# Down projection by 2x2 block products in seven pairs of the first half, with the rest rows' low parts on GpSimd

## The chip, the cores and the metric

The kernel runs on one core of a Trainium2 chip. The time is that of one execution on the device, in microseconds (us); the median of three runs is compared. The engines are named as in the profile: PE is TensorE, DVE VectorE, ACT ScalarE, POOL GpSimd, SP the engine that issues most transfers. PEld is PE's loading of weights.

## The reference

Two branches read the same x (2048 tokens, 576 features) and are mixed by a gate for each token. All is float32.

```python
def _B_ref(x, W_gate, W_up, W_down):            # 576 -> 4608 -> 576
    gate = jnp.einsum("bsd,df->bsf", x, W_gate)
    up = jnp.einsum("bsd,df->bsf", x, W_up)
    gate = gate * (lambda x, dt: x.astype(dt))(gate > 0, gate.dtype)
    h = gate * up
    return jnp.einsum("bsf,fd->bsd", h, W_down)

x = A_x
g = _sigmoid((x * gate_w).sum(-1, keepdims=True))
a = _A_ref(x, A_wqkv, A_w_phi, A_wo)            # linear attention with 32 heads
b = _B_ref(x, B_W_gate, B_W_up, B_W_down)
return g * a + (1 - g) * b
```

The change lies in branch B, the gated layer: two projections up to 4608 features, a product, and the down projection back to 576.

## The kernel before

**Precision.** A float32 operand is split into a high part (rounded by ACT to the type that PE takes at full rate) and a low part (the difference, made by DVE: source minus high part). A product is then three matmuls: high by high, high by low, low by high.

**Stages.** The first 340 us of the span or so are attention. Then come 72 units, and a short tail. The 4608 features are 36 chunks of 128; the tokens are two halves of 1024, each of two blocks t of 512. Units 0 to 35 take the chunks with the first half's tokens, units 36 to 71 with the second's (`units`, L855). Two units with neighbouring chunks are a pair g; there are NG = 18 pairs in a half. Unit u belongs to pair u // 2; the first unit of a pair is called even, the second odd.

**A unit** makes gate and up for one chunk and 1024 tokens by seven block products in place of eight (Strassen's scheme in Winograd's form), on pre-added operands. `step(u, j)` (L1322 and on) issues one of them: `product` puts seven 512-column matmuls on a bank of PSUM, in the order 1, 5, 6, 2, 7, 3, 4 for j = 0 to 6. The text counts steps from 1, so product 4 is step 7. Products 1, 6, 7, 4 accumulate one after another on a bank cx, 5 and 3 on ca, 2 on cy, and between them ACT and DVE read the running sums: ACT copies cx and ca aside (g1, u2, g2), DVE adds cy, cx and ca to the copies (L1413, L1415, L1418; L1415 is the add of cx to u2, which has to be over before product 4 goes on the same bank), and `gated` (L1290) makes h from gate and up, one block of 512 tokens at a time.

**The weights of the products** are made in the first half, one unit ahead (`make` in `step`), and stored in HBM for the second half. For unit v = u + 1: ACT makes the high parts of three weight blocks (L864, in `blocks`) at j = 0, DVE their low parts (L867, 128x768) and the low part of the rest rows (`low_w_rows`, L870, 32 partitions x 384) at j = 1; at j = 2 DVE adds the blocks up in place in four instructions (`sums_of_blocks`, L885 to L888), which have to wait for the readers of the old values; ACT makes those sums' high parts at j = 3, DVE the low parts (L867 128x1024 and L870 32x512) at j = 4. SP stores the two tiles at j = 2 and j = 5 (L1393, L1400). In the second half SP loads them again instead.

**The down projection** of pair q is issued while pair q + 1 is computed: after the product of step j, `step` appends the s-th down product, s = 7 * odd + j. It lands on one of two banks, pd0 and pd1, in turn, and DVE adds the bank to the sums in SBUF one step later (`add_up`). The output's 576 features are four blocks of 128, taken as i, m, and 64 rest rows on banks of their own (pm).

- First half, plain (`plain_down`, `down_plain`): eight products of two chunks by three matmuls, and the rest rows in 8 matmuls. Each of the pair's four hidden blocks (two chunks, two token blocks) has a high part (`high_h`, L1233) and a low part (`low_h`, L1238). The pair's weights come in with `load_down` (L908), and their parts are made in its odd unit, at j = 2 and 3 (L1091, L1094).
- Second half but for its last pair, by blocks (`prepare_down`, `down`): for each m seven products of the 2x2 block scheme with three matmuls each, and the rest rows in 8 matmuls. The hidden blocks and their differences (`minus`, L1287) make seven operands, each with a high and a low part; the weights' blocks are added up by POOL in place (`down_sums_of_blocks`, L1080 to L1083) and split in two steps for each m, m = 0 in the pair's odd unit and m = 1 in the next even one. After each of the 14 products DVE adds the bank to a sum (L1206).

**Other work on DVE in the first half.** `second_half` scales the second half's tokens and adds up their operands on DVE, one instruction of 128x768 (L335, L341) at the end of each unit from unit 4, until it is done.

**Order.** `in_order` around the units holds PE, DVE, ACT, POOL and SP to the order in which `step` issues. Within a step it is: the product, the add of the last down product, the hidden parts, the weights for the next unit, the copies and adds of gate and up, the down weights, the next down product.

Of the kernel before, what the change touches and what calls it, by code (L numbers as in the profile page):

```python
# [7 lines left out]
F32 = mybir.dt.float32  # L8
# [75 lines left out]
def gated_mix_kernel(  # L84
# [26 lines left out]
    SUB, ADD, MULT = ALU.subtract, ALU.add, ALU.mult  # L111
    tt, pt = nc.vector.tensor_tensor, nc.gpsimd.tensor_tensor
# [98 lines left out]
    with tc.tile_pool(name="ps_v", bufs=1, space=PSUM) as ps_v:  # L211
# [7 lines left out]
        for k in range(5):  # L219
            w = raw.tile([P, TB + VW], F32, name="xwv", tag="raw")  # L220
# [428 lines left out]
    t = NT - 1  # L649
# [203 lines left out]
    NG = NC // 2  # L853
# [3 lines left out]
    def load_w(u):  # L857
        if units[u][0] == 0:
            RAW[u] = wraw.tile([P, 4, 3, P], F32, name="wr")
            nc.sync.dma_start(RAW[u], wgu[units[u][1]])  # L860
# [5 lines left out]
    def low_w(o, a):  # L866
        tt(out=o[:, :, 3:5], in0=a[:, :, 0:2], in1=o[:, :, 0:2].bitcast(F32), op=SUB)  # L867

    def low_w_rows(o, a):
        tt(out=o[64:96, :, 2], in0=a[64:96, :, 2], in1=o[64:96, :, 2].bitcast(F32), op=SUB)  # L870

    WB, WS = {}, {}

    def blocks(u, f):

        if u not in WB:
            o = WB[u] = wop.tile([P, 3, 5, P], F32R, name="wb")
            WO[u] = {1: (o, 0), 2: (o, 1), 4: (o, 2)}
        f(WB[u], RAW[u][:, 0:3])
# [10 lines left out]
    def block_sums(u, f):  # L890
        if u not in WS:
            o = WS[u] = wop.tile([P, 4, 5, P], F32R, name="ws")
            WO[u].update({5: (o, 2), 6: (o, 0), 7: (o, 3), 3: (o, 1)})
        f(WS[u], RAW[u])
# [164 lines left out]
    WD, W4, HID, ACC, ACC4, BANK, REST = {}, {}, {}, {}, {}, {}, {}  # L1059
# [36 lines left out]
    def rest_weights(g, step):  # L1096

        a = WDR[g][:, 8 * P:].rearrange("p (c q) -> p c q", c=2)
        if step == 0:
            nc.scalar.activation(W4[g][:, 0:2, 0], a, AF.Copy)  # L1100
        elif step == 1:
            tt(out=W4[g][:, 0:2, 1], in0=a, in1=W4[g][:, 0:2, 0].bitcast(F32), op=SUB)
            pt(out=a[:, 0], in0=a[:, 0], in1=a[:, 1], op=ADD)
        elif step == 2:
            nc.scalar.activation(W4[g][:, 2, 0], a[:, 0], AF.Copy)
            nc.scalar.activation(W4[g][:, 3], W4[g][:, 1].bitcast(F32), AF.Copy, scale=-1.0)
        else:
            tt(out=W4[g][:, 2, 1], in0=a[:, 0], in1=W4[g][:, 2, 0].bitcast(F32), op=SUB)
# [21 lines left out]
    def rows(i, m, t, hf):  # L1130
        r = (2 * i + m) * P
        return slice(r, r + P), slice((2 * hf + t) * TB, (2 * hf + t + 1) * TB)
# [5 lines left out]
    def load_rest(hf):  # L1138
        for t in range(2):
            a = ACC4[hf, t] = sums_of[t][:64, 2]  # L1140
            nc.sync.dma_start(a, att[4 * P:, rows(0, 0, t, hf)[1]])

    PLAIN = {1: (0, 0, 1), 2: (0, 1, 1), 3: (2, 0, 1), 4: (0, 0, 0), 5: (0, 1, 0), 6: (2, 0, 0),
             8: (1, 0, 1), 9: (1, 1, 1), 11: (1, 0, 0), 12: (1, 1, 0)}

    def down_plain(g, s):

        if s not in PLAIN:
            return lambda: []
        i, m, t = PLAIN[s]  # L1150
        first, last = g == 0, g == NG - 1
# [25 lines left out]
            return []  # L1177
        return add

    def down(g, s, bank):  # L1180

        first, last = g == NG, g == 2 * NG - 2
        m, i = divmod(s, 7)
        n = DOWN[i]
        key = 0 if n in (1, 6, 7, 4) else 1
        if n in (1, 5, 2):
            BANK[m, key] = bank(m, n)
        ps = BANK[m, key]
        h, l = HID[g, n]
        o, k = WD[g, m], PLACE[n]  # L1190
        mm = lambda ps, w, v, a, z: nc.tensor.matmul(ps, w, v, start=a, stop=z, skip_group_check=True)  # L1191
        mm(ps, o[:, 0, k], h, n in (1, 5, 2), False)
        mm(ps, o[:, 0, k], l, False, False)
        mm(ps, o[:, 1, k], h, False, True)
        if m == 0 and n in (1, 5, 2, 4):
            w, r = {1: (0, 0), 5: (2, 1), 2: (1, 0), 4: (3, 1)}[n]
            if first and n in (1, 5):
                REST[r] = pm.tile([P, TB], F32, name=f"pm{r}")
            w = W4[g][:, w].rearrange("p s q -> p (s q)")
            mm(REST[r], w, h, first and n in (1, 5), False)  # L1200
            mm(REST[r], w, l, False, last and n in (2, 4))

        def add():
            i, t = ADDS[n]
            a = ACC[1, i, m, t]
            tt(out=a, in0=ps, in1=a, op=ADD)  # L1206
            return []
        return add
# [22 lines left out]
    def high_h(key, src):  # L1231
        h, l = hp.tile([P, TB], F32R, name="hh"), hp.tile([P, TB], F32R, name="hl")
        nc.scalar.activation(h, src, AF.Copy)  # L1233
        HID[key] = h, l

    def low_h(key, src):
        h, l = HID[key]
        tt(out=l, in0=src, in1=h.bitcast(F32), op=SUB)  # L1238
# [34 lines left out]
    def add_up():  # L1273

        if len(STORED) > 2:
            for hf, i, m, t in STORED.pop(0):
                if hf == 0:
                    load_acc(1, i, m, t)
        if PEND:
            done.extend(PEND.pop()())  # L1280
        store(done)
        STORED.append(tuple(done))
        done.clear()

    def minus(a, b):

        tt(out=b, in0=a, in1=b, op=SUB)  # L1287
# [11 lines left out]
    def bank(n):  # L1299

        pool, name, new = {1: (px, "cx", 1), 6: (px, "cx", 0), 7: (px, "cx", 0), 4: (px, "cx", 0),
                           5: (pa, "ca", 1), 3: (pa, "ca", 0), 2: (py, "cy", 1)}[n]
        if new:
            BANKS[name] = pool.tile([P, TB], F32, name=name)
        return BANKS[name], bool(new)
# [16 lines left out]
    def step(u, j):  # L1322


        g, odd = divmod(u, 2)
        v, q = u + 1, g - 1
        plain, was_plain = g < NG or g == 2 * NG - 1, q < NG
        ps, first = bank(SEQ[j])
        product(ps, u, SEQ[j], first)
        add_up()  # L1330
        make = 0 < u < NC - 1
        cx, ca, cy = (BANKS.get(n) for n in ("cx", "ca", "cy"))
        old = not odd and g > 0

        if j == 0:
            if u > 0:
                last_cx, a = LATE.pop()
# [5 lines left out]
        e2, e1, o2, o1 = ODD[q] if old else EVEN[g] + (None, None) if odd else [None] * 4  # L1343
        if odd and plain or old and was_plain:
            key, x2, x1 = ((g, 0), e2, e1) if odd else ((q, 1), o2, o1)
            if j == 0:
                high_h(key + (1,), x2)
            elif j == 1:
                high_h(key + (0,), x1)
                low_h(key + (1,), x2)  # L1350
            elif j == 2:
                low_h(key + (0,), x1)
        elif odd:
            if j == 1:
                high_h((g, 1), e1)
            elif j == 3:
                low_h((g, 1), e1)
                minus(e2, e1)
            elif j == 4:
                high_h((g, 5), e1)  # L1360
            elif j == 5:
                low_h((g, 5), e1)
        elif old:
            if j == 0:
                high_h((q, 6), e1)
                minus(o2, e2)
            elif j == 1:
                high_h((q, 3), o2)
                low_h((q, 6), e1)
            elif j == 2:  # L1370
                low_h((q, 3), o2)
                high_h((q, 7), e2)
                high_h((q, 2), o1)
            elif j == 3:
                minus(o1, e1)
                low_h((q, 7), e2)
            elif j == 4:
                high_h((q, 4), e1)
                low_h((q, 2), o1)
            elif j == 5:  # L1380
                low_h((q, 4), e1)

        if make:
            if j == 0:
                blocks(v, high_w)
                if v + 1 < NC:
                    load_w(v + 1)
            elif j == 1:
                blocks(v, low_w)
                blocks(v, low_w_rows)  # L1390
            elif j == 2:
                if v < NC - 2:
                    nc.sync.dma_start(wbd[v], WB.pop(v).bitcast(F32))  # L1393
                sums_of_blocks(v)
            elif j == 4:
                block_sums(v, low_w)
                block_sums(v, low_w_rows)
            elif j == 5:
                if v < NC - 2:
                    nc.sync.dma_start(wsd[v], WS.pop(v).bitcast(F32))  # L1400
        elif j == 0 and NC < u < 2 * NC - 1:
            load_operands(v)
# [13 lines left out]
        elif j == 6:  # L1416
            a = T["g2"]
# [5 lines left out]
            w = WO.pop(u)  # L1423
# [9 lines left out]
            prepare_down(g, 0, j)  # L1433
        elif old and not was_plain:
            prepare_down(q, 1, j)
        if old and j == 5:
            load_down(g)
        if old and j == 6:
            ODD.pop(q)
# [26 lines left out]
                store_rest(0, 1)  # L1466
                load_rest(1)
        if j == 6 and u < NC:
            if u >= 4:
                next(later_half, None)  # L1470
            if u == NC - 3:
                for _ in later_half:
                    pass
                load_operand(1, 0)
                load_operand(1, 1)

    later_half = second_half()
    with in_order(tc, nc, nc.tensor, nc.vector, nc.scalar, nc.gpsimd, nc.sync):
# [4 lines left out]
        g = 2 * NG - 1  # L1483
# [149 lines left out]
```

## Time and profile before

| | |
|---|---|
| median of three runs | 1589.73 us (1588.61 to 1591.07) |
| profiled execution | 1589.56 us, its span 1587.8 us |
| granted TensorE clock | 0.997 |
| DVE busy in one pair of the first half (440.60 to 475.50 us of the span) | 27.93 of 34.90 us |
| DVE busy in one pair of the second half (1099.15 to 1132.70 us) | 24.82 of 33.55 us |
| POOL busy in the same two stretches | 0.00 and 4.31 us |

A row of a timeline or of the chain begins with its start and its length in us, counted from the span's start. Then come the engine, the line of the kernel, the operation, what it writes and reads (a tile's number is left out, so that cx stands for all its buffers), the shapes and the count. In square brackets stand the engine's idle time just before and what ended it. A row of a group of instructions has the count, then the total busy time in us and the mean of one in ns, then the idle time before them. An engine's instructions are pipelined: the next one starts before the recorded end of the last, so the time from start to start is what an instruction costs in a queue.

### The profile page before, as it was taken

What the parts mean: (1) busy time and instruction counts of PE and PEld (TensorE: products, weight loads), DVE (VectorE), ACT (ScalarE), POOL (GpSimd) and SP (SyncE); (2) the same over time, 40 slices, a digit from 0 to 9 for tenths busy, and PEclk for the clock granted to TensorE, in tenths of its full rate; (3) what the DMA queues carried; (4) which work ended last, traced back from release to release, by engine and by line L of the source; (5) the groups of instructions that cost most, each with busy time, mean ns of one, the idle gap of its engine ahead of it and who ended that gap; (6) DMA issues with size and microseconds to landing.
All of it is one profiled execution on the core that took longest, in us unless ns stands there. A gap on an engine that the chain in (4) does not pass through costs nothing.

```text
span 1587.8 us, 20181 instructions
## 1 busy us (share of the span) xinstructions
PE 1570.8 (99%) x7823; PEld 1313.4 (83%) x7823; DVE 1190.8 (75%) x1865; ACT 559.0 (35%) x918; POOL 175.2 (11%) x243
## 2 busy tenths in 40 slices
PE   9999999999999999999999999999999999999998
PEld 9999995677888888888888888888888888888887
DVE  4997774577778777787777777777777777777777
ACT  4344335554333333333333334232233232222321
POOL 0126521110000000000000002111111111111110
PEclk9999999999999999999999999999999999999999
DMA  5365315587655576555554516543343343443432
GB/s 171 108 207 192 143 55 157 170 332 261 217 219 211 209 262 223 215 191 221 193 196 183 210 71 233 189 177 143 143 180 143 146 175 131 167 168 131 180 140 75
DMA packets 64539, 283.38 MB, mean 178 GB/s; under 512 B 6802, under 2 KB 17298, under 8 KB 55740
## 3 DMA queue, kind: packets, MB, share of 16 engines
q1 hardware_dynamic: 61228, 270.34, 47.0%
q0 software_dynamic: 2352, 10.11, 2.0%
q10 hardware_dynamic: 864, 1.65, 0.3%
q8 instruction: 61, 1.00, 0.3%
q14 instruction: 34, 0.28, 0.0%
HBM read 172.07 MB, written 108.60 MB: 177 GB/s over the span
## 4 chain that ended last, share of the span: by engine, by line
PE 95%; DVE 3%; ACT 1%; DMA 0%; issue 0%; POOL 0%; SPq 0%; ACTq 0%; POOLq 0%
PE cx L1128 29%; PE ca L1128 14%; PE pd L1168 12%; PE pd L1191 10%; PE cy L1128 7%; PE kv L175 4%; PE pk L175 3%; PE pq L175 3%; PE pm L1168 2%; PE pm L1191 2%; PE kv L421 1%; PE po L562 1%; PE pv L237 1%; PE pw L175 1%; PE ptr L379 1%; PE psf L259 1%
## 5 line engine op out<-in xcount | busy, mean ns | idle before, releaser
L1233 ACT ACTIVATE hh<-g 128x512 fp32r<-128x512 f32 x195 | 120.0, 624 | 458.5 <-DVE g L1290 289.2
L1206 DVE TENSOR_TENSOR ac<-pd,ac 128x512 f32<-128x512 f32 x238 | 164.1, 689 | 144.0 <-PE pd L1191 143.9
L1128 PE MATMUL cx<-xo,ws 128*128 128x512 f32 x1008 | 253.5, 391 | 3.3 <-ACT g L1294 3.3
L1128 PE MATMUL ca<-xo,ws 128*128 128x512 f32 x1008 | 251.9, 389 | 0.0
L1128 PE MATMUL cx<-xo,wb 128*128 128x512 f32 x1008 | 249.0, 389 | 1.5 <-DVE u L1415 1.5
L1128 PEld LDWEIGHTS cx<-xo,ws 128*128 128x128 f32 x1008 | 190.2, 189 | 43.3 <-ACT g L1294 3.7
L1128 PEld LDWEIGHTS cx<-xo,wb 128*128 128x128 f32 x1008 | 188.2, 188 | 42.5 <-DVE u L1415 1.9
L1128 PEld LDWEIGHTS ca<-xo,ws 128*128 128x128 f32 x1008 | 189.2, 188 | 39.3
L1168 PE MATMUL pd<-hh,wd 128*128 128x512 f32 x576 | 200.7, 389 | 0.0
L1191 PE MATMUL pd<-hh,wd 128*128 128x512 f32 x476 | 185.2, 389 | 0.0
L1174 DVE TENSOR_TENSOR ac<-pd,ac 128x512 f32<-128x512 f32 x144 | 99.1, 688 | 105.8 <-PE pd L1168 103.3
L1238 DVE TENSOR_TENSOR hl<-g,hh 128x512 fp32r<-128x512 f32 x195 | 135.7, 696 | 1.9 <-ACT hh L1233 0.2
L1294 ACT ACTIVATE g<-cx 128x512 f32<-128x512 f32 x144 | 85.0, 590 | 130.8 <-PE cx L1128 130.7
L1128 PE MATMUL cy<-xo,wb 128*128 128x512 f32 x504 | 127.3, 392 | 0.0
L1168 PEld LDWEIGHTS pd<-hh,wd 128*128 128x128 f32 x576 | 108.1, 188 | 22.6
L1091 ACT ACTIVATE wd<-wdr 128x384 fp32r<-128x384 f32 (+1 forms) x106 | 62.3, 606 | 143.4 <-DMA wdr<-wd 143.4
L1128 PEld LDWEIGHTS cy<-xo,wb 128*128 128x128 f32 x504 | 95.6, 190 | 20.0
L1168 PE MATMUL pd<-hl,wd 128*128 128x512 f32 x288 | 112.0, 389 | 0.0
L1191 PEld LDWEIGHTS pd<-hh,wd 128*128 128x128 f32 x476 | 89.3, 188 | 18.6
L1191 PE MATMUL pd<-hl,wd 128*128 128x512 f32 x238 | 92.6, 389 | 0.0
L831 POOL TENSOR_TENSOR xo<-xr,xo 32x512 fp32r<-32x512 f32 x5 | 8.3, 1669 | 615.9 <-ACT xo L847 615.9
L864 ACT ACTIVATE ws<-wr 128x1536 fp32r<-128x1536 f32 x36 | 53.7, 1491 | 46.6 <-DVE wr L888 46.6
(256 smaller groups left out, 2574.1 us busy)
## 6 DMA issues: line engine op xcount, KB each, us to landing
wsd<-ws SPq DMA_DIRECT2D x34, 1280.0 KB
ws<-wsd SPq DMA_DIRECT2D x34, 1280.0 KB
wbd<-wb SPq DMA_DIRECT2D x34, 960.0 KB
wb<-wbd SPq DMA_DIRECT2D x34, 960.0 KB
wr<-wgu SPq DMA_DIRECT2D x36, 768.0 KB
wdr<-wd SPq DMA_DIRECT2D x36, 576.0 KB
eT<-et SPq DMA_DIRECT2D x10, 594.0 KB
xt<-xb SPq DMA_DIRECT2D x7, 768.0 KB
```

Of the source, the lines that this page charges most:

```text
L175: nc.tensor.matmul(ps, w, m, start=i == 0, stop=i == len(pairs) - 1)
L237: nc.tensor.matmul(pv[i][c], m, w_[:, k, cs], start=k == 0 and n == 0, stop=k == 4 and n == 1)
L864: nc.scalar.activation(o[:, :, 0:3], a, AF.Copy)
L1091: nc.scalar.activation(o[:, 0], a, AF.Copy)
L1128: nc.tensor.matmul(ps, w, v, start=first and m == 0, stop=m == len(pairs) - 1, skip_group_check=True)
L1168: nc.tensor.matmul(ps, w, v, start=k == 0 and (i < 2 or first), stop=k == len(mms) - 1 and (i < 2 or last), skip_group_check=True)
L1174: tt(out=a, in0=ps, in1=a, op=ADD)
L1191: mm = lambda ps, w, v, a, z: nc.tensor.matmul(ps, w, v, start=a, stop=z, skip_group_check=True)
L1206: tt(out=a, in0=ps, in1=a, op=ADD)
L1233: nc.scalar.activation(h, src, AF.Copy)
L1238: tt(out=l, in0=src, in1=h.bitcast(F32), op=SUB)
L1294: nc.scalar.activation(a, ps, AF.Copy)
```

## The change

Pairs 3, 5, 7, 9, 11, 13 and 15 of the first half (`BY_BLOCKS`) take the down projection by blocks, as the second half does; the pairs between them stay plain. The rest rows keep their plain form in the first half: a table `REST_OF` names the down product with which a rest matmul pair goes, the weights' slot and the hidden operand, and the one operand that the seven lack for it (the even chunk's second token block) gets a high and a low part of its own, under the key 8.

In the odd unit of such a pair and in the two units after it, GpSimd makes the low parts of the product weights' rest rows (L870) in place of DVE. DVE's sums of the blocks and SP's stores then wait for GpSimd.

The load of such a pair's down weights is issued at j = 1 of its even unit in place of j = 5; for the plain pair after it, it stays at j = 5, behind the blocks pair's last low part of down weights, which reads the same tile. `second_half` skips the unit after a pair by blocks.

```diff
-    def low_w_rows(o, a):
-        tt(out=o[64:96, :, 2], in0=a[64:96, :, 2], in1=o[64:96, :, 2].bitcast(F32), op=SUB)
+    def low_w_rows(o, a, f=tt):
+        f(out=o[64:96, :, 2], in0=a[64:96, :, 2], in1=o[64:96, :, 2].bitcast(F32), op=SUB)
+
+    def low_w_rows_aside(o, a):
+        low_w_rows(o, a, pt)
...
             tt(out=W4[g][:, 0:2, 1], in0=a, in1=W4[g][:, 0:2, 0].bitcast(F32), op=SUB)
-            pt(out=a[:, 0], in0=a[:, 0], in1=a[:, 1], op=ADD)
+            if g >= NG:
+                pt(out=a[:, 0], in0=a[:, 0], in1=a[:, 1], op=ADD)
+        elif g < NG:
+            return
...
+    BY_BLOCKS = range(3, NG - 2, 2)
+
+    def is_plain(g):
+        return g < NG and g not in BY_BLOCKS or g == 2 * NG - 1
...
+    REST_OF = ({1: (0, 0, 1), 5: (0, 1, 8), 3: (1, 1, 3), 2: (1, 0, 2)},
+               {1: (0, 0, 1), 5: (2, 1, 5), 2: (1, 0, 2), 4: (3, 1, 4)})
...
-        if m == 0 and n in (1, 5, 2, 4):
-            w, r = {1: (0, 0), 5: (2, 1), 2: (1, 0), 4: (3, 1)}[n]
+        rest = REST_OF[g // NG]
+        if m == 0 and n in rest:
+            w, r, i = rest[n]
+            h, l = HID[g, i]
...
-            a = ACC[1, i, m, t]
+            a = ACC[g // NG, i, m, t]
...
-        plain, was_plain = g < NG or g == 2 * NG - 1, q < NG
+        plain, was_plain = is_plain(g), is_plain(q)
...
+        rows_ = low_w_rows_aside if g in BY_BLOCKS and odd or q in BY_BLOCKS else low_w_rows
...
         elif odd:
+            if g < NG and j < 2:
+                (high_h, low_h)[j]((g, 8), e2)
...
-                blocks(v, low_w_rows)
+                blocks(v, rows_)
...
-                block_sums(v, low_w_rows)
+                block_sums(v, rows_)
...
-        if old and j == 5:
+        if old and j == (1 if was_plain and not plain else 5):
             load_down(g)
...
-            if u >= 4:
+            if u >= 4 and not (old and q in BY_BLOCKS):
                 next(later_half, None)
```

## The prediction

> **What bounds the kernel now.** I read the page first, then who waited for whom, the chain that ended last, and last the timelines of the engines in single pairs.
>
> ```profile
> span 1587.8 us, 20181 instructions
> PE 1570.8 (99%) x7823; PEld 1313.4 (83%) x7823; DVE 1190.8 (75%) x1865; ACT 559.0 (35%) x918; POOL 175.2 (11%) x243
> ```
>
> TensorE (PE) is busy 99% of the span, so whole matmuls taken out of it are worth time, if nothing comes in their place. The chain shows what a matmul is worth (start, length, what), in one pair of the first half:
>
> ```profile
> 404.37 3.17 PE cx L1128 x14
> 407.54 1.59 PE ca L1128 x7
> 409.12 1.36 PE pd L1168 x6
> ...
> 439.27 3.17 PE cx L1128 x14
> ```
>
> The same place comes back after 34.90 us, which are 98 matmuls of products and 56 of the down projection: 0.2266 us each. PE never pauses between. In all 72 units its timeline has two pauses, both in the first two; the second is this row:
>
> ```profile
> 369.16 3.02 PE L1128 MATMUL cx<-xo,wb 128*128 128x512 f32 x12 [1.51 <-DVE u L1415]
> ```
>
> That is the end of unit 1, where a unit lasts 49 matmuls and VectorE (DVE) has two units' worth of weights to make: PE waited 1.51 us, because product 4 (step 7) accumulates on the bank that the add of L1415, "the u add" below, must read first. DVE is in order, so whatever stands before the u add in its queue can hold up PE. That is the wait I follow.
>
> **PE's side of the change.** A plain pair takes 8x6 matmuls and 8 for the rest rows; by blocks it is 14x3 and again 8: 50, six less. Six matmuls are 1.36 us (the pd row above), seven pairs 9.5 us. The second half, which runs by blocks already, confirms it:
>
> ```profile
> 1099.43 0.69 DVE L1290 SCALAR_TENSOR_TENSOR g<-g,u 128x512 f32<-128x512 f32 x1
> ...
> 1133.00 0.69 DVE L1290 SCALAR_TENSOR_TENSOR g<-g,u 128x512 f32<-128x512 f32 x1
> ```
>
> 33.57 us from pair to pair, 1.33 less than 34.90. But there DVE makes no weights for the products.
>
> **DVE's side.** These rows give the prices, in the even and odd unit of a plain pair:
>
> ```profile
> 456.76 0.69 DVE L1174 TENSOR_TENSOR ac<-pd,ac 128x512 f32<-128x512 f32 x1 [1.66 <-PE pd L1168]
> 457.37 0.68 DVE L1418 TENSOR_TENSOR g<-ca,g 128x512 f32<-128x512 f32 x1
> 458.09 0.69 DVE L1290 SCALAR_TENSOR_TENSOR g<-g,u 128x512 f32<-128x512 f32 x1
> 458.69 0.95 DVE L335 TENSOR_TENSOR xb<-xb,ac 128x768 f32<-128x768 f32 x1
> 459.56 0.68 DVE L1290 SCALAR_TENSOR_TENSOR g<-g,cx 128x512 f32<-128x512 f32 x1
> ...
> 463.79 0.69 DVE L1174 TENSOR_TENSOR ac<-pd,ac 128x512 f32<-128x512 f32 x1 [1.51 <-PE pd L1168]
> 464.40 0.68 DVE L1238 TENSOR_TENSOR hl<-g,hh 128x512 fp32r<-128x512 f32 x1
> 465.00 0.55 DVE L885 TENSOR_TENSOR wr<-wr 128x384 f32<-128x384 f32 x1
> ...
> 467.25 0.68 DVE L1174 TENSOR_TENSOR ac<-pd,ac 128x512 f32<-128x512 f32 x1
> 467.85 1.42 DVE L1094 TENSOR_TENSOR wd<-wdr,wd 128x1024 fp32r<-128x1024 f32 x2
> 469.18 1.22 DVE L867 TENSOR_TENSOR ws<-wr,ws 128x1024 fp32r<-128x1024 f32 x1
> ```
>
> From start to start, 512 columns take 0.60 us (0.72 when the next one reads the result: 457.37 to 458.09), 768 take 0.87, the four chained sums 2.25 (465.00 to 467.25), the low parts of a plain pair's weights, 1024 and 128, 1.33 (467.85 to 469.18). On the same line lie 384 at 0.47 and 1024 at 1.14. A result is there 0.09 after its slot.
>
> A pair by blocks gives DVE four more low parts (8 for 4), four differences and six more adds, 14 instructions of 0.60, and lower parts of 2x384, 2x512 and 128 columns (2.3 us) in place of 1.33: some 9.4 us. It falls into three units, A (the pair's odd one), B (the next pair's even one) and C (its odd one); a plain even unit D closes the cycle. PE gives them 73, 78, 70 and 81 matmuls: 16.54, 17.68, 15.86, 18.36 us, 68.45 in place of 69.81.
>
> Taken off DVE in A, B and C are the two rest-row instructions of each unit:
>
> ```profile
> L870 DVE TENSOR_TENSOR ws<-wr,ws 32x512 fp32r<-32x512 f32 x36 | 24.6, 684 | 0.5
> L870 DVE TENSOR_TENSOR wb<-wr,wb 32x384 fp32r<-32x384 f32 x36 | 19.8, 550 | 0.5
> ```
>
> ```profile
> 463.59 1.75 PE L1128 MATMUL cx<-xo,ws 128*128 128x512 f32 x7
> ```
>
> That is 1.23 us a unit. The u adds now, first without GpSimd (POOL) in the way:
>
> - A: its last step's queue is add, add, gated, difference and the second half's 768: 4x0.60+0.87 and two dependent waits of 0.11, 3.5 us. It starts when PE has done the down product before the seventh product, 66 matmuls or 14.96 us into A, and 0.20 later (PE's next product at 463.59, DVE's add at 463.79). 18.66 is 2.11 past the end of A. A's own u add stands before that and is in time.
> - B: DVE comes in 2.11 late and never gets a pause. Up to and with the u add it has 15 instructions of 512 (9.0), 768, 384, four sums and 1024 (0.87+0.47+2.25+1.14): 13.7 us. The u add is done at 15.9, and PE sees it 0.06 later, as in unit 1. PE is there after 68 matmuls, at 15.41. Wait: 0.6.
> - C: DVE caught up. From step 3's add, which waits for PE until 4.73 (20 matmuls and 0.20), 7x0.60, the sums 2.25, the plain weights 1.33 and 1024: 8.9; done and seen at 13.8, PE there at 13.60. Wait: 0.2.
> - D has the old load and PE's longest steps. No wait.
>
> So 0.8 of the 1.36 us goes back before POOL does anything: 0.57 gained a cycle, 4.0 us in all.
>
> **POOL's side.** POOL gets six rest-row instructions a cycle and the block sums of the down weights, which A and B did not have. Their nearest rows, and DVE beside three of them:
>
> ```profile
> L1080 POOL TENSOR_TENSOR wdr<-wdr 128x128 f32<-128x128 f32 x34 | 15.7, 462 | 240.6 <-DVE wd L1094 240.6
> ```
> ```profile
> 967.16 1.28 POOL L831 TENSOR_TENSOR xo<-xr,xo 32x512 fp32r<-32x512 f32 x1 [3.90 <-ACT xo L847]
> 969.68 1.29 POOL L831 TENSOR_TENSOR xo<-xr,xo 32x512 fp32r<-32x512 f32 x1 [1.25 <-ACT xo L847]
> 971.58 4.46 POOL L831 TENSOR_TENSOR xo<-xr,xo 32x512 fp32r<-32x512 f32 x2 [0.61 <-ACT xo L847]
> ```
> ```profile
> 967.20 2.33 DVE L851 TENSOR_TENSOR xo<-xo 128x1024 fp32r<-128x1024 f32 x1
> 969.45 0.68 DVE L1174 TENSOR_TENSOR ac<-pd,ac 128x512 f32<-128x512 f32 x1
> 970.05 1.47 DVE L1238 TENSOR_TENSOR hl<-g,hh 128x512 fp32r<-128x512 f32 x1
> 971.45 1.21 DVE L851 TENSOR_TENSOR xo<-xo 128x1024 fp32r<-128x1024 f32 x1
> 972.58 0.68 DVE L1174 TENSOR_TENSOR ac<-pd,ac 128x512 f32<-128x512 f32 x1
> ```
>
> A row instruction of 512 takes POOL 1.28 us, one of 384 by the line between 0.46 (128) and 1.28 some 1.0, a sum 0.46: 4.1 us in A and in B, 2.3 in C. They do not run beside DVE. The 1024 of L851, 1.21 us undisturbed (971.45), took 2.33 when POOL began 0.04 before it: it was held until 0.12 before POOL's end (968.44). The low part at 970.05 took 1.47 for 0.69, held in the same way. POOL's two from 971.58 took 4.46 instead of 2.56, so the later one of the two engines waits. The add from PSUM at 972.58, with POOL running, took its normal 0.68. So DVE instructions with both inputs in SBUF (low parts, sums, differences) exclude POOL's, the adds from banks do not. Bounds of what POOL costs DVE: nothing, if all fall beside adds from banks or pauses, and 4.1 in B and 2.3 in C, if none does.
>
> ```profile
> 467.36 1.49 ACT L864 ACTIVATE ws<-wr 128x1536 fp32r<-128x1536 f32 x1 [1.32 <-DVE wr L888]
> ```
>
> I placed them. B: the row instruction of 384 follows ScalarE's high parts, at 3.2 after the unit's start; DVE is in a bank add, then the next low part is held 0.24. The four sums are ready when DVE's own four stand in its queue, two held engines taking turns: three are held, by 0.30, 0.19 and 0.19. The 512, ready when ScalarE has made the sums' high parts in 1.49 us (the row above), meets a low part: held 0.52. In all 1.45. C: the 384 finds DVE waiting for PE and costs nothing; the 512 is ready at 9.9, waits for the 1024 of the plain weights and then holds the 128 behind it by 1.12. A: held too, but A's u add had half a microsecond to spare and PE's adds pace the rest. So PE waits 0.6+1.45 in B and 0.2+1.12 in C, 3.36 a cycle, against 1.36 saved: 2.0 us lost a cycle, 14.0 us in all.
>
> The rule of the Trainium skill on page "SBUF — State Buffer", section "Who interferes with whom", says that a VectorE instruction with two SBUF inputs and a GpSimd instruction that reads SBUF exclude each other, the loser blocked for the whole instruction, and that one with at most one SBUF input is untouched. The rows agree, but for the last 0.12 us; by its wording the six held instructions of B and C would lose 0.12 more each, 0.72 a cycle, and the estimate would be 1608.6 us.
>
> **The rest costs nothing, with its cover.** ScalarE gets four more high parts of 512 columns and more weights in a pair, and is 35% busy. The load of the down weights that moves from step 6 to step 2 of a blocks pair's even unit passes two stores of weights on SP's queue, which nobody reads in this half. SP's stores wait for POOL's rows in place of DVE's, a microsecond or two later, with a half of the kernel to spare; POOL itself has nothing else in these units.
>
> **Sum.** The profiled execution took 1589.56 us (span 1587.8), 0.17 under the median. 1589.56 - 9.5 + 7x3.36 = 1603.6 us. With half or one and a half of the 2.57 us of collisions it is 1594.6 or 1612.6: this case's own range.
>
> **Rivals.** (1) Faster: POOL's instructions slip into DVE's pauses, or DVE's queue drains earlier than I laid it out, so that the u add is in time in B and C. For it: DVE is idle a quarter of the span, and the second half shows POOL's sums beside a full blocks load without a pause of PE. Against: B has no DVE pause. It decides at 1.36 us of waits a cycle: below, the change gains. No collisions give 1585.6, no waits at all 1580.0. (2) The gain is cancelled within 0.2% (3.2 us, about what a measurement here can tell from no change): collisions of 0.1 to 1.0 us a cycle in place of 2.57, 1586.4 to 1592.8. (3) Slower still: the plain pair's load, now behind B's late last low part on SP's queue, comes after ScalarE needs it in C, and the copies of banks queue up behind it.
>
> ```profile
> 1014.18 0.33 SPq L908 DMA_DIRECT2D wdr<-wd  x1
> ```
> ```profile
> 1017.55 0.53 ACT L1091 ACTIVATE wd<-wdr 128x384 fp32r<-128x384 f32 x1 [7.94 <-DMA wdr<-wd]
> ```
>
> It lands 3.4 us after its issue in the second half; issued some 18 us into B it is there 2 us into C, and PE feels it only from 7 on. Each microsecond over that costs 7 us; with the exclusion longer than I took it, 1614 and above.
>
> **Chances.** Forecast 0.62; faster 0.13, of which half near 1585.6; cancelled 0.12; slower still 0.13. Faster by over 0.2% 0.13, within 0.12, slower 0.75. The range 1585 to 1614 takes in the bound without collisions and one and a half of them, and leaves out the full gain and most of the last case.
>
> **What would show it.** PE's pauses in the first half stand at cx with releaser DVE u L1415, about 2 us in B and 1.3 in C, from pair 3 on; L867, L1238 and L885 to L888 grow longer than 0.95, 0.69 and 0.56 where POOL runs; pairs 4, 6 and so on last over 34.9 us. If PE has no pauses there, or waits for ScalarE or a DMA, I am wrong.

## The result: 1% slower

The changed kernel takes 1604.74 us in the median (1603.22 to 1606.01), the kernel before 1589.55 us in the same session; the ratio is 1.0096 [1.0081, 1.0112]. The forecast was 1603.6 us. The profiled execution took 1603.22 us, 13.66 more than that of before. From its page:

```profile
span 1601.4 us, 20439 instructions
PE 1565.1 (98%) x7781; PEld 1303.4 (81%) x7781; DVE 1259.8 (79%) x1942; ACT 581.6 (36%) x967; POOL 260.0 (16%) x341
L1134 PE MATMUL cx<-xo,wb 128*128 128x512 f32 x1008 | 253.3, 393 | 20.6 <-DVE u L1434 20.6
```

PE has lost 42 matmuls (7823 to 7781) and is busy 5.7 us less, yet the span is 13.6 longer. The last row says where PE stood idle: ahead of the products on cx, for 20.6 us where the same group of before had 1.5, and always for the u add (L1415 before, L1434 here). Its place is where the forecast put it, in B and C. PE's timeline in the cycle of pair 3, B and then C:

```profile
491.01 1.88 PE L1134 MATMUL cx<-xo,wb 128*128 128x512 f32 x7 [1.71 <-DVE u L1434]
...
508.30 1.88 PE L1134 MATMUL cx<-xo,wb 128*128 128x512 f32 x7 [1.13 <-DVE u L1434]
```

The brackets count from the recorded end of the last matmul. From start to start, less the spacing of 0.2266 us, B's pause is 1.87 us (488.92 to 491.01) and C's 1.29; below, a pause is always counted so.

To keep the other parts of the kernel out, I use one **stretch**: from the u add of unit 6 to that of unit 34, which holds the seven cycles whole. Its two ends, in before and in the changed kernel:

```profile
454.42 0.68 DVE L1415 TENSOR_TENSOR u<-cx,u 128x512 f32<-128x512 f32 x1
...
943.12 0.68 DVE L1415 TENSOR_TENSOR u<-cx,u 128x512 f32<-128x512 f32 x1
```
```profile
452.52 0.68 DVE L1434 TENSOR_TENSOR u<-cx,u 128x512 f32<-128x512 f32 x1
...
956.86 0.68 DVE L1434 TENSOR_TENSOR u<-cx,u 128x512 f32<-128x512 f32 x1
```

488.70 us became 504.34, 15.6 more. After the stretch nothing differs (622.99 us to the u add of unit 71 in both); ahead of it the changed kernel's execution is 1.9 us quicker, and not by the change: before's ran at half clock for a while where the units begin (see the last section). 15.6 less 1.9 is the 13.7 between the two executions.

### The profile page after: what moved, and what is told of

Read it like the earlier page. It is cut to its first block, busy times and chain, and to the rows that moved or that the text cites. A ratio compares the mean times of both kernels' runs of the same rounds, so it can differ in the third digit from the quotient of the medians.

```text
span 1601.4 us, 20439 instructions
## 1 busy us (share of the span) xinstructions
PE 1565.1 (98%) x7781; PEld 1303.4 (81%) x7781; DVE 1259.8 (79%) x1942; ACT 581.6 (36%) x967; POOL 260.0 (16%) x341
## 4 chain that ended last, share of the span: by engine, by line
PE 81%; DVE 14%; issue 2%; ACT 1%; DMA 1%; POOL 0%; SPq 0%; DVEq 0%; ACTq 0%; POOLq 0%
PE cx L1134 25%; PE ca L1134 12%; PE pd L1205 11%; PE pd L1179 7%; PE cy L1134 6%; PE kv L175 4%; PE pk L175 3%; PE pq L175 3%; DVE ac L1222 2%; DVE hl L1254 2%; PE pm L1205 2%; PE pm L1179 1%; DVE ws L867 1%; PE kv L421 1%; PE po L562 1%
## 5 line engine op out<-in xcount | busy, mean ns | idle before, releaser
L1222 DVE TENSOR_TENSOR ac<-pd,ac 128x512 f32<-128x512 f32 x336 | 230.7, 687 | 156.1 <-PE pd L1205 154.4
L1249 ACT ACTIVATE hh<-g 128x512 fp32r<-128x512 f32 x223 | 137.0, 625 | 452.8 <-DVE g L1306 226.2
L1134 PE MATMUL cx<-xo,wb 128*128 128x512 f32 x1008 | 253.3, 393 | 20.6 <-DVE u L1434 20.6
L1254 DVE TENSOR_TENSOR hl<-g,hh 128x512 fp32r<-128x512 f32 x223 | 158.8, 712 | 0.7 <-ACT hh L1249 0.2
L1205 PEld LDWEIGHTS pd<-hh,wd 128*128 128x128 f32 x672 | 126.4, 188 | 26.3
L1205 PE MATMUL pd<-hl,wd 128*128 128x512 f32 x336 | 131.0, 390 | 0.0
L1094 ACT ACTIVATE wd<-wdr 128x384 fp32r<-128x384 f32 (+1 forms) x120 | 69.3, 588 | 133.2 <-DMA wdr<-wd 133.2
L1185 DVE TENSOR_TENSOR ac<-pd,ac 128x512 f32<-128x512 f32 x88 | 60.5, 687 | 55.6 <-PE pd L1179 50.8
L870 POOL TENSOR_TENSOR wb<-wr,wb 32x384 fp32r<-32x384 f32 x21 | 24.6, 1174 | 382.4 <-ACT wb L864 250.2
L1097 DVE TENSOR_TENSOR wd<-wdr,wd 128x384 fp32r<-128x384 f32 (+1 forms) x120 | 84.5, 712 | 0.0
L1179 PEld LDWEIGHTS pd<-hh,wd 128*128 128x128 f32 x352 | 66.1, 188 | 14.2 <-DVE ac L1185 0.4
L1205 PEld LDWEIGHTS pd<-hl,wd 128*128 128x128 f32 x336 | 63.2, 188 | 13.3
```

What stands on the lines that cost most here:

```text
L870: f(out=o[64:96, :, 2], in0=a[64:96, :, 2], in1=o[64:96, :, 2].bitcast(F32), op=SUB)
L1094: nc.scalar.activation(o[:, 0], a, AF.Copy)
L1097: tt(out=o[:, 1], in0=a, in1=o[:, 0].bitcast(F32), op=SUB)
L1134: nc.tensor.matmul(ps, w, v, start=first and m == 0, stop=m == len(pairs) - 1, skip_group_check=True)
L1179: nc.tensor.matmul(ps, w, v, start=k == 0 and (i < 2 or first), stop=k == len(mms) - 1 and (i < 2 or last), skip_group_check=True)
```

## The experiments

**The theories.** T, that of the forecast: PE waits for the u add, because DVE's queue ahead of it has grown, by DVE's own new work and by the time for which POOL's instructions hold DVE's. Rivals: R1, moving the rows to POOL does the harm, and undoing it brings the gain back; R2, the waits are cancelled or caused elsewhere (PE's scheme itself, the banks, ScalarE, the plain load of rival 3), so that no order of DVE's work helps.

All edits are to the changed kernel. Times against the kernel before, run on the same chip; the stretch against before's; B and C are PE's pauses ahead of product 4 of these units in one cycle, two values where the cycles with an instruction of `second_half` at the end of A (four) and without (three) differ:

| kernel | us | ratio | stretch | B | C |
|---|---|---|---|---|---|
| changed kernel | 1604.74 | 1.0096 | +15.6 | 1.87 / 1.63 | 1.29 |
| e1, rows on DVE | 1612.2 | 1.0139 [1.0122, 1.0156] | +22.0 | 2.25 / 1.77 | 1.50 |
| e3, no rows | 1588.44 | 0.999 [0.9981, 0.9999] | -0.2 | 1.01 / 0.56 | 0.19 |
| e4, no rows, no sums | 1584.81 | 0.997 [0.9959, 0.9981] | -4.1 | 0.58 / 0 | 0.19 |
| e5, u add first | 1594.58 | 1.0025 [1.0014, 1.0036] | +6.0 | 0.68 / 0.44 | 1.32 |
| e2, rows on POOL, no blocks | 1589.47 | 1.0 [0.9991, 1.0009] | 0.0 | 0 | 0 |
| e6, no sums | 1595.49 | 1.0039 [1.0026, 1.0052] | +5.6 | 1.31 / 1.05 | 0.69 |
| e7, reordered | 1582.75 | 0.9961 [0.9948, 0.9973] | -6.4 | 0 | 0 |
| e8, e7's order, no blocks | 1588.36 | 0.9996 [0.9987, 1.0005] | 0.0 | 0 | 0 |
| e9, e7 with rows on POOL | 1585.46 | 0.9971 [0.9962, 0.998] | -3.8 | 0 | 0.35 |

**e1: the rows back on DVE**

```diff
-        rows_ = low_w_rows_aside if g in BY_BLOCKS and odd or q in BY_BLOCKS else low_w_rows
+        rows_ = low_w_rows
```

> The blocks pairs stay, the rest rows' low parts go back to VectorE everywhere. Theory (the u add comes late because VectorE has more to do AND is excluded by GpSimd): VectorE gains 1.23 us of work a unit and loses about the same in holds, so the waits of a cycle stay about 3.4 us (2.3 in unit B, 1.1 in C) and the time stays within 2 us of the changed kernel's 1604.7 us. Rival 1 (VectorE's load alone, GpSimd's work is free): two units of a cycle get 1.23 us later, 17 us in all, 1622 us. Rival 2 (the move to GpSimd is what costs, the blocks alone gain): below 1587 us.

1612.2 us, slower still: R1 fell at once, and T's number was missed by 7.5 us as well. In DVE's timeline of e1, B of pair 3:

```profile
480.00 0.95 DVE L867 TENSOR_TENSOR wb<-wr,wb 128x768 fp32r<-128x768 f32 x1
480.96 0.55 DVE L870 TENSOR_TENSOR wb<-wr,wb 32x384 fp32r<-32x384 f32 x1
481.54 0.56 DVE L1097 TENSOR_TENSOR wd<-wdr,wd 128x384 fp32r<-128x384 f32 x1
...
489.02 1.22 DVE L867 TENSOR_TENSOR ws<-wr,ws 128x1024 fp32r<-128x1024 f32 x1
490.25 0.68 DVE L870 TENSOR_TENSOR ws<-wr,ws 32x512 fp32r<-32x512 f32 x1
490.97 0.69 DVE L1432 TENSOR_TENSOR g<-cy,g 128x512 f32<-128x512 f32 x1
```

The two rows take slots of 0.58 and 0.72, and the two instructions ahead of them 0.1 more each than without them (480.00 to 480.96 for 0.87): 1.5 us a unit on DVE. On POOL the rows hold DVE by 0.78 in B and 1.11 in C (worked out further below; the sums hold it in both kernels, by nearly the same), so the move to POOL saves DVE 0.7 us in B and 0.4 in C, and the pauses get only some 0.5 us a cycle shorter (24.7 against 21.4 in the stretch). The rest of e1's 6.3 us more are shorter pauses at other matmuls and a clock that was halved twice where the changed kernel has it once.

**e3 and e4: what POOL's work costs.** e3 leaves out the rest rows' low parts in A, B and C; e4 also the block sums of the down weights in the first half.

```diff
+        rows_ = (lambda o, a: None) if g in BY_BLOCKS and odd or q in BY_BLOCKS else low_w_rows
...
     def down_sums_of_blocks(g, m):
+        if g < NG:
+            return
```

> The changed kernel with the rest rows' low parts of the product weights left out in units A, B and C of the seven pairs (that part of the computation is missing). Theory: GpSimd's holds in B fall to those of its block sums (about 0.7 us), in C to none; waits of 1.3 and 0.2 us a cycle against 1.36 saved, so about 1590 us, no change against the kernel before, with up to 1.5 us for PE's restarts after its waits. Rival 1 (VectorE's load alone): nothing changes, 1604 us. Rival 3 (a transfer or ScalarE holds PE): nothing changes, 1604 us.

> As the kernel without rest rows, and GpSimd's block sums of the down weights left out in the first half as well (both parts of the computation are missing), so that GpSimd does nothing in these units. Theory: only VectorE's own load is left, waits of 0.6 us in B and 0.2 us in C, 0.57 us gained a cycle: 1585.5 us, with 1.5 us for restarts 1587. Rival 1 and rival 3: 1604 us, as before the omission.

1588.44 and 1584.81: T's numbers, but 1.6 and 0.7 us lower. The groups of the products on cx in e3 and e4:

```profile
L1134 PE MATMUL cx<-xo,wb 128*128 128x512 f32 x1008 | 252.2, 391 | 6.3 <-DVE u L1434 6.1
```
```profile
L1136 PE MATMUL cx<-xo,wb 128*128 128x512 f32 x1008 | 251.8, 391 | 3.4 <-DVE u L1436 3.2
```

With POOL silent in these units, 1.9 us by the count of the last row are left beside the 1.5 of unit 1 (3.7 from start to start). So POOL's work costs the changed kernel 19.9 us against not being done at all (1604.74 to 1584.81; 1.6 of the difference between the two stretches is a halving of the clock, see the last section), and DVE's own new work little. In e4, B waits only in the four cycles in which the last step of A has a 128x768 instruction of `second_half`.

**e6: without the sums alone**

```diff
     def down_sums_of_blocks(g, m):
+        if g < NG:
+            return
```

> The changed kernel with GpSimd's block sums of the down weights left out in the first half (that part of the computation is missing), the rest rows on GpSimd as in the changed kernel. Theory: in B the holds of VectorE's four sums go (0.7 us a cycle), in C nothing changes: 5 us less than the changed kernel, 1600 us. If the sums and the rows held VectorE independently, the two omissions apart would add up to that of both; the kernel without both is 20 us under the changed one and the one without rows 16.

1595.49: 9 us less than the changed kernel where 5 were expected. Of the 10.0 us by which the stretch is shorter, 1.6 are the halving of the clock that e6 does not have. C had no sums to lose, and yet its pause fell from 1.29 to 0.69. POOL and DVE there, first in the changed kernel and then in e6:

```profile
503.29 1.28 POOL L870 TENSOR_TENSOR ws<-wr,ws 32x512 fp32r<-32x512 f32 x1 [6.93 <-ACT ws L864]
```
```profile
502.20 2.52 DVE L1097 TENSOR_TENSOR wd<-wdr,wd 128x1024 fp32r<-128x1024 f32 x2
504.64 0.68 DVE L1222 TENSOR_TENSOR ac<-pd,ac 128x512 f32<-128x512 f32 x1
505.24 1.21 DVE L867 TENSOR_TENSOR ws<-wr,ws 128x1024 fp32r<-128x1024 f32 x1
```
```profile
504.99 1.43 POOL L870 TENSOR_TENSOR ws<-wr,ws 32x512 fp32r<-32x512 f32 x1 [7.03 <-ACT ws L864]
```
```profile
503.86 1.41 DVE L1099 TENSOR_TENSOR wd<-wdr,wd 128x1024 fp32r<-128x1024 f32 x2
505.19 0.68 DVE L1224 TENSOR_TENSOR ac<-pd,ac 128x512 f32<-128x512 f32 x1
505.79 1.71 DVE L867 TENSOR_TENSOR ws<-wr,ws 128x1024 fp32r<-128x1024 f32 x1
```

In the changed kernel POOL starts at 503.29; the 128-column low part could start at 503.34 (502.20 and a slot of 1.14) and is held until POOL's end: the two together take 2.44 in place of 1.33. In e6 the two start within 0.01 us of each other (504.99), and it is the low part that goes through: POOL's record is 0.15 longer, DVE goes on with an add from a bank, which POOL does not touch, and the next low part is held by only 0.5 (1.71 for 1.21). The Trainium skill, page "SBUF — State Buffer", section "Who interferes with whom", says that the order of issue decides which of the two blocks; these rows agree. So the two omissions do not add up (rows 16.3, sums 9.2, both 19.9): each one shifts where the other's instructions fall.

**e5: the u add ahead of what it can pass.** The add is issued right behind the product of step 6, ahead of the bank add and, in B, a low part.

```diff
         product(ps, u, SEQ[j], first)
+        if j == 5:
+            tt(out=T["u2"], in0=BANKS["cx"], in1=T["u2"], op=ADD)
         add_up()
...
-        elif j == 5:
-            tt(out=T["u2"], in0=cx, in1=T["u2"], op=ADD)
```

> The changed kernel with one move in VectorE's order in every unit: the u add is issued at the start of step 6, ahead of the bank add and the low part of that step. Theory: it is 1.2 us earlier in B; in C, where it passes one add, the row instruction then holds the low weights as before and the gain is nearly nothing. Waits 0.7 us in B (plus a new 0.2 us for a low part) and 1.4 us in C: 1595.5 us, 1597 with restarts, so 7 to 9 us less than the changed kernel. Rival 3 (a transfer or ScalarE holds PE): no change, 1604 us.

1594.58, a microsecond below the range. Without touching any work, two instructions fewer ahead of the u add took B's pause from 1.87 to 0.68: its queue is the cause. C gained nothing, though its u add passes an add as well. DVE's timeline of e5 shows why:

```profile
497.13 1.77 DVE L867 TENSOR_TENSOR wb<-wr,wb 128x768 fp32r<-128x768 f32 x1
498.83 0.68 DVE L1222 TENSOR_TENSOR ac<-pd,ac 128x512 f32<-128x512 f32 x1
```

The row instruction of 384, harmless to C in the changed kernel, now starts 0.5 ahead of this low part (POOL's record is 496.59 to 498.08) and holds it 0.8.

**e2: the other half of the change alone.** No pair goes by blocks; POOL makes the rows in the same 21 units.

```diff
-    BY_BLOCKS = range(3, NG - 2, 2)
+    BY_BLOCKS = ()
+    ASIDE = range(3, NG - 2, 2)
```

> All pairs of the first half plain again; GpSimd makes the rest rows' low parts in the same 21 units (and the second half's work skips the same units). Theory: GpSimd's instructions hold VectorE's as in the changed kernel, some 1 to 2 us a unit, but here VectorE has pauses of more than that before each u add, so PE waits nowhere and the time is that of before, 1589.7 us within 2 us. Rival (the move to GpSimd costs by itself, through the sums and the stores that now wait for it): 2 to 9 us slower.

1589.47 against 1589.36, the stretch the same to 0.01 us. POOL's rows hold DVE here too, but its queue has room. DVE in e2:

```profile
477.58 1.77 DVE L867 TENSOR_TENSOR wb<-wr,wb 128x768 fp32r<-128x768 f32 x1
...
484.79 1.23 DVE L867 TENSOR_TENSOR ws<-wr,ws 128x1024 fp32r<-128x1024 f32 x1 [0.96 <-ACT ws L864]
```

The first is held by 0.8, and at the second DVE has 0.96 to spare.

**e7, e8, e9: another order.** If only the place in DVE's queue matters, the low parts of the added blocks need not stand ahead of the u add. e7 has e5's edit, the rows on DVE, those low parts of B and C behind the u add, and `second_half`'s instructions in D, where DVE has room.

```diff
+        late = q in BY_BLOCKS
...
-                blocks(v, rows_)
+                blocks(v, low_w_rows)
...
-            elif j == 4:
-                block_sums(v, low_w)
-                block_sums(v, rows_)
+            elif j == 4 and not late:
+                low_parts(block_sums, v)
             elif j == 5:
+                if late:
+                    low_parts(block_sums, v)
...
+        if u < NC and (j == 6 and 4 <= u < 7 or j in (0, 3, 6) and u > 7 and old and g in BY_BLOCKS):
+            next(later_half, None)
```

> A version from what the runs showed, nothing left out: the u add at the start of step 6; the rest rows on VectorE; in B and C both low parts of the block sums' weights (1024 and 512 columns, 1.9 us) behind the u add; the second half's instructions taken out of A, B and C and put three at a time into D, where VectorE has pauses. Theory: what stood between PE's product and the u add is down to what fits, waits of some 0.8 us a cycle in place of 3.3, against 1.36 saved: 4 us less than the kernel before, 1585.5 us, if no new wait (a low part of a hidden block that comes too late for the down product, a copy of ScalarE's) takes more than 0.5 us a cycle. Rival (the exclusion is symmetric, so each order of the same work gives the same waits): 1600 us or more.

e8 is e7 with all pairs plain (`BY_BLOCKS` empty, the conditions of the order kept), e9 is e7 with the rows on POOL in A, B and C as in the changed kernel.

> The reordered version with all pairs of the first half plain: the order alone, without block products. Theory: PE has no wait in the first half's plain pairs that the order could remove, so the time is that of before within 1.5 us, and the whole gain of the reordered version comes from the matmuls. Rival (the order alone gains, by DVE finishing earlier): 2 us or more below the kernel before.

> The reordered version with the rest rows' low parts on GpSimd again in A, B and C. Theory: VectorE loses 1.5 us of work in each of these units but is held at arbitrary places before the u add and the hidden blocks' low parts; 4 us more than the reordered version, about that of the kernel before, 1587 to 1590 us. Rival (taking work off VectorE always helps where it is the engine that is late): 1580 us, PE's full saving.

e7 takes 1582.75 us, 0.9961 [0.9948, 0.9973]: faster than both kernels, 2.8 us below what was expected, and R2 fell. Its page and its DVE timeline in B of pair 3:

```profile
L1134 PE MATMUL cx<-xo,wb 128*128 128x512 f32 x1008 | 249.9, 389 | 1.5 <-DVE u L1347 1.5
```
```profile
490.51 0.68 DVE L1347 TENSOR_TENSOR u<-cx,u 128x512 f32<-128x512 f32 x1
491.11 0.68 DVE L1222 TENSOR_TENSOR ac<-pd,ac 128x512 f32<-128x512 f32 x1
491.71 0.68 DVE L1254 TENSOR_TENSOR hl<-g,hh 128x512 fp32r<-128x512 f32 x1
492.31 1.22 DVE L867 TENSOR_TENSOR ws<-wr,ws 128x1024 fp32r<-128x1024 f32 x1
```

The 1024 that stood ahead of the u add stands behind it, and the group's idle time is before's 1.5 again. One pause of 0.28 us in a cycle is left, at product 6 of C (cx from xo and ws, 499.71), which has to wait for ACT's copy of cx. ACT's queue in e7:

```profile
496.96 0.63 ACT L1249 ACTIVATE hh<-g 128x512 fp32r<-128x512 f32 x1 [7.36 <-DVE g L1306]
...
499.07 0.58 ACT L1310 ACTIVATE g<-cx 128x512 f32<-128x512 f32 x1
```

The copy ends 0.06 before the product starts, and from ACT's wait for DVE's `gated` on ACT does not idle: what was put behind the u add delays what stands behind it. No run tests that by itself. DVE is busy 1258.9 us, as much as in the changed kernel (1259.8): what counted was the order. e8 shows no change, so the gain is that of the matmuls and not of the order alone. e9 gives 2.7 us back, short of the 4 expected and below its range of 1587 to 1590, but in T's direction. The intervals of the two ratios overlap; that e9 is the slower one rests on the stretch, 2.5 us longer, and on the pauses: 0.35 in C where e7 has none, and 0.14 in place of 0.28 at product 6 of C. With the queue in good order, POOL's rows still cost more than they free. In e9, B:

```profile
480.13 1.77 DVE L867 TENSOR_TENSOR wb<-wr,wb 128x768 fp32r<-128x768 f32 x1
...
488.69 1.23 DVE L1254 TENSOR_TENSOR hl<-g,hh 128x512 fp32r<-128x512 f32 x1
```

Both are held, by 0.8 and 0.55. What each of e7's other moves does was not separated.

## Why the prediction was right, point by point

**PE's saving, 9.5 us:** right. The stretch has 2156 matmuls before and 2114 after, 42 of 0.2266 us.

**DVE's lateness out of A, 2.11 us:** right. PE's first product of B is the eighth matmul of the row below, 472.12 + 7x0.2266 = 473.71; DVE comes to the first instruction behind A's last step at 475.84, 2.13 later. PE and DVE of the changed kernel:

```profile
472.12 3.11 PE L1134 MATMUL cx<-xo,wb 128*128 128x512 f32 x13
```
```profile
474.97 0.95 DVE L335 TENSOR_TENSOR xb<-xb,ac 128x768 f32<-128x768 f32 x1
475.84 0.68 DVE L1306 SCALAR_TENSOR_TENSOR g<-g,cx 128x512 f32<-128x512 f32 x1
...
477.64 0.90 DVE L1254 TENSOR_TENSOR hl<-g,hh 128x512 fp32r<-128x512 f32 x1
478.47 0.94 DVE L867 TENSOR_TENSOR wb<-wr,wb 128x768 fp32r<-128x768 f32 x1
...
481.01 0.81 DVE L888 TENSOR_TENSOR wr<-wr 128x384 f32<-128x384 f32 x1
481.85 0.70 DVE L889 TENSOR_TENSOR wr<-wr 128x384 f32<-128x384 f32 x1
482.59 0.70 DVE L890 TENSOR_TENSOR wr<-wr 128x384 f32<-128x384 f32 x1
483.32 0.56 DVE L891 TENSOR_TENSOR wr<-wr 128x384 f32<-128x384 f32 x1
...
486.20 1.22 DVE L1254 TENSOR_TENSOR hl<-g,hh 128x512 fp32r<-128x512 f32 x1
487.35 1.21 DVE L867 TENSOR_TENSOR ws<-wr,ws 128x1024 fp32r<-128x1024 f32 x1
```

**DVE's own waits, 0.6 in B and 0.2 in C:** right where they can be seen alone. e4 has 0.58 and 0.19; but its B waits in only four of seven cycles, those with an instruction of `second_half` at the end of A, and the forecast counted all seven.

**POOL's holds, 1.45 in B and 1.12 in C:** right in place and nearly in size. By slots from start to start in the rows above, the low part at 477.64 takes 0.83 (held 0.23; forecast 0.24), the three sums 0.84, 0.74 and 0.73 where the same sums take 0.59 in C (held 0.25, 0.15 and 0.14; forecast 0.30, 0.19 and 0.19), the low part at 486.20 takes 1.15 (0.55; forecast 0.52). That is 1.32 in B. In C the two low parts at 502.20 take 2.44 for 1.33: 1.11. In POOL's timeline the holders:

```profile
476.85 1.14 POOL L870 TENSOR_TENSOR wb<-wr,wb 32x384 fp32r<-32x384 f32 x1 [8.67 <-ACT wb L864]
480.03 0.47 POOL L1083 TENSOR_TENSOR wdr<-wdr 128x128 f32<-128x128 f32 x1 [2.03 <-DVE wd L1097]
480.57 0.83 POOL L1084 TENSOR_TENSOR wdr<-wdr 128x128 f32<-128x128 f32 x1
...
485.59 1.29 POOL L870 TENSOR_TENSOR ws<-wr,ws 32x512 fp32r<-32x512 f32 x1 [2.71 <-issue]
495.34 1.01 POOL L870 TENSOR_TENSOR wb<-wr,wb 32x384 fp32r<-32x384 f32 x1 [8.46 <-ACT wb L864]
```

The taking of turns shows in 0.83 for a sum of 0.47. The 384 of C (495.34) falls on DVE's pause and costs nothing, as the forecast had it.

That fits the four cycles of this kind. In the three without `second_half` at the end of A, the pause of B came out 0.4 short of the forecast (1.63 for 2.05) by two errors that partly offset each other. DVE has 0.87 less to do in A, so that its own 0.58 turns into 0.29 to spare; but the 384 then meets the longer low part of 768. In B of pair 7 POOL's starts at 620.66, and DVE has:

```profile
621.17 1.77 DVE L867 TENSOR_TENSOR wb<-wr,wb 128x768 fp32r<-128x768 f32 x1
```

That is a hold of 0.82 in place of 0.23. The holds are 1.92 there; less 0.29 that is 1.63, the pause measured.

C's hold is a matter of 0.05 us, as e6 shows, where 0.5 came of it. That its size came out is partly luck.

**The pauses, 3.36 us a cycle:** 3.16 in the four cycles with `second_half` in A (1.87 + 1.29; one has 1.91), 2.92 in the three others; 21.4 in all against 23.5.

**What the sum lacked.** Two terms of the other sign, and together with the pauses they close the account of the stretch: the second matmul behind each pause comes 0.11 late (14 times, 1.5 us), and one halving of the clock cost 1.6; -9.5 + 21.4 + 1.5 + 1.6 = 15.0, and the last 0.6 lie in 109 spacings, each within 4 us of a pause or of the halving, that are 0.001 to 0.014 us wider. So 1603.6 came 1.1 from the median in part because the forecast's pauses were 2.1 too large and those terms were missing.

**The rule on the exclusion.** By the wording of the Trainium skill, page "SBUF — State Buffer", section "Who interferes with whom", held instructions would have lost 0.12 more each. The measured holds are those of the rows, or less; the shorter price was the right one.

**The rivals.** (1) and (2) fell: the pauses are there in every cycle. e4 is (1) brought about by leaving work out: 1584.81 us where 1585.6 was worked out for no collisions. (3) fell: ACT had the plain weights' load in time in C, with no wait in the brackets of this row:

```profile
498.02 1.25 ACT L1094 ACTIVATE wd<-wdr 128x1024 fp32r<-128x1024 f32 x2
```

## What to carry to other kernels

When an engine that idles a quarter of the span gets more work, look at which instruction in its queue the bound engine waits for, and put the new work behind that one before trying to move work elsewhere: here the order was worth 19 us (the changed kernel against e9), while the offloading gained 7.5 us in all under the poor order (e1 against the changed kernel, 1.6 of it one halving of the clock less) and lost 2.7 under the good one. Work moved to GpSimd is not gone from VectorE if it reads SBUF while VectorE runs instructions with both inputs in SBUF; it comes back as holds whose size depends on hundredths of a microsecond. An experiment that takes work out shifts all these meetings, so that its difference is no clean price of what it took out.

## What the hardware showed beside that

**A pause can cost the clock.** In the changed kernel, PE's pause of 1.91 us in the cycle of pair 11 was followed by this (stretch, its length, busy time and count of PE, PEld, DVE, ACT and POOL, then the granted clock, DMA share and GB/s):

```profile
780.00:784.00 4.00, 4.00 (x12) 3.13 (x12) 2.15 (x4) 1.69 (x2) 1.00 (x1) 0.60 0.98 329
784.00:788.00 4.00, 4.00 (x19) 3.27 (x19) 2.94 (x5) 2.52 (x4) 0.00 (x0) 1.00 0.06 23
```

The granted clock fell to 0.60 for this stretch, and 12 matmuls fell into it, some in part, in place of 19; it cost 1.6 us. Of e1's four pauses of 2.25 us two had the same effect; none of 1.87 us or less had it, and the stretches of before, e2 and e8, which have no pause, have no halving. The length of the pause alone does not decide: where the units begin, PE pauses for 3.44 us in every kernel here, and in ten of the eleven executions the clock was halved behind it, in the changed kernel's not. First before, then the changed kernel:

```profile
348.00:352.00 4.00, 4.00 (x11) 3.09 (x10) 2.78 (x4) 1.58 (x3) 0.55 (x1) 0.50 0.99 415
```
```profile
348.00:352.00 4.00, 4.00 (x19) 3.27 (x19) 3.87 (x6) 1.88 (x4) 0.05 (x1) 1.00 0.99 416
```

The Trainium skill, page "TensorE: Matmul & The Clock Gate", section "What's actually happening", gives half clock after at least one idle window of about 3.4 us. By that, pauses of 2 us would be free of it; here they were not always. What decides, perhaps where the pause falls against a window that the trace does not show, stays open.
